# Working the later rows of the first batch before its earlier rows in a fused attention and two-MoE kernel

## The chip, the cores and the metric

The kernel runs on one core of a Trainium2 chip. The metric is the device time of one execution in microseconds (us); three executions of the kernel before were timed, and their median is the figure to compare with. Engines are called by the profile's names: PE is TensorE (PEld its weight loads), DVE is VectorE, ACT is ScalarE, POOL is GpSimd, SP is SyncE, whose queue issues most DMAs.

## What is computed

Four batches of attention over 8 heads, 576 rows and 64 columns a head, are followed by two MoE layers of 2304 rows, width 512 and inner width 2048.

```python
scores = scale * q @ k.T                  # causal: row i sees keys 0..i
local = softmax(scores) @ v
q_p = phi(q)                              # phi(x) = (x if x > 0 else exp(x) - 1) + 1
mem_out = (q_p @ M_prev) / (q_p . z_prev + 1e-6)
attn = sigmoid(beta) * mem_out + (1 - sigmoid(beta)) * local
x1 = silu(attn_rows @ w_in) @ w_out       # MoE 1
x2 = elu(x1 @ w2_in) @ w2_out             # MoE 2
```

The weights come as 64-bit floats.

## The kernel before, in words

**Attention.** The work of a batch is cut by pairs of heads (`NP` = 4 pairs) and by rows. Region "A" is rows 0 to 255 and needs keys 0 to 255; region "B" is rows 256 to 575 and needs all 576 keys. Batch 0 works A and B as tasks of their own (`tasks`, line 664), four A tasks and then four B tasks; batches 1 to 3 have tasks "AB" that do both. A task first loads q, k, v, the rows of q for the memory part, z and M (`load`), then makes its softmax (`soft`, called with "A", "23" or "4": the tiles of 128 rows, `wide` gives how many keys each sees) and its memory part (`mem_soft`), and, one task later in the program's order, turns the probabilities round on PE (`a_T`, `b_T`, into tile `a`), multiplies with v (`av_mm`) and ends with `av_end`, whose copy `pt<-av` is the last ACT instruction of a task and whose DMA writes the result to DRAM (`xdA`, `xdB`). In `soft`, ACT makes the exponentials with their sums, and for the tiles of region B also the scaling (`NORM`); for tile A the scaling is DVE's. Scores go into PSUM banks: tag "s" has two, and for the A tasks, which run only in batch 0, one bank is that of an accumulator ("acc0" or "acc1") of the MoE, which is not at work yet. Tiles `e3` and `e4` have one buffer a head, `eA` and `e2` two.

**MoE 1.** A block is 256 rows (all of "A", or two strips of 128 of "B"; the 64 rows left over of each batch make block "T"). Its x is read back from DRAM (`x_load`, tile `stg`) and cut in a high and a low part (`x`), so that three matmuls make one product of full precision. Eight steps j make the inner columns, two tiles of 128 each: `gemm1` writes `h`, ACT and DVE make `t` and `g`, `gemm2` adds into acc0 and acc1. The 32 weight tiles (16 of w_in, 16 of w_out, one of each by turns) are loaded with 512 KB each and decoded on ACT and DVE from 64-bit words (`w_value`, `w_split`: two ACT and four DVE instructions a tile); step j needs four of them. So that each decoded weight is used at once by two blocks, the first two blocks are worked in halves: block (0,A) with steps 0 to 3, block (0,B) with steps 0 to 3, (0,A) with steps 4 to 7, (0,B) with steps 4 to 7, and then block (1,A) whole. A block can't start before the last `av_end` of its region.

**Order.** All instructions are recorded first, and a planner (`Plan.order`) then sorts them: list scheduling forward and backward by turns with its own costs, and the best pass is taken. The program's order sets the first pass's priorities and, through the rotation of the tiles' buffers, a part of the dependences: q, k, v, z and M of a task go to buffers that an earlier task must have left. The first eight tasks have a bonus in priority (`BOOST`). When attention is over its buffers are given to the second part: the other six MoE 1 blocks in pairs, and MoE 2.

All instructions have line L199 (the planner's call), so groups are told apart by tile names. `h<-mask` are 70 filler matmuls of no use to the result.

Of the kernel before, what the change touches and what calls it, by code (L numbers as in the profile page):

```python
# [26 lines left out]
LAST = 3  # L27
# [361 lines left out]
def attention_moe_moe_kernel(  # L389
# [16 lines left out]
    B, H, D, S = qT.shape  # L406
    DM, DFF = w1_in.shape
    NF = DFF // 128
    NP = H // 2
# [20 lines left out]
    def new(pool, shape, dtype, tag, bufs=1):  # L430
        return nc.tile(pool, shape, dtype, tag, bufs, "psum" if pool is PP else "sbuf")

    def bank(tag, bufs=1):
        return new(PP, [128, 512], F32, tag, bufs)
# [226 lines left out]
        nc.vector.tensor_copy(pair[0:64, :], fv[0:64, :, 0])  # L661
        nc.vector.tensor_copy(pair[64:128, :], fv[64:128, :, 1])

    tasks = [(b, p, r) for b in range(B) for r in (("AB",) if b else ("A", "B")) for p in range(NP)]
    qk_t, pr_t, e_t, pq_t, pt_t = {}, {}, {}, {}, {}
    x_done = set()

# [42 lines left out]
    def scores(task, parts):  # L710

        rq, rk = qk_t[task]
        mm2([(outs[u], rq[u * 64:u * 64 + 64, q0:q1], rk[u * 64:u * 64 + 64, k0:k1], True, True)
             for outs, q0, q1, k0, k1 in parts for u in range(2)])

    def masked(o, s, m0, init, acc):
        m = mask[:, m0:m0 + o.shape[1]]
        nc.vector.tensor_tensor_reduce(out=o, in0=s, in1=m, scale=-scale, scalar=init,
                                       op0=ALU.add, op1=ALU.min, accum_out=acc)

    def soft(task, nms):


        b, p, rg = task
        heads = range(1 if nms == "4" else 2)
        k = 1 if nms == "4" else 2
        small = new(at, [128, 8], F32, f"sm{nms}", 2)
        mx, su = small[:, 0:4], small[:, 4:8]
        tiles = []
        for nm in nms:  # L730
            e = [new(at, [128, wide[nm]], F32, f"e{nm}{u}", 2 if nm in EDUP else 1) for u in heads]
            for u in heads:
                e_t[task, u, nm] = e[u]
            if nm == "4":
                ss, cn = [bank("s", 2) for _ in range(2)], ((0, 384), (384, 192))
                scores(task, [([s[0:64, 0:n], s[64:128, 0:n]], 512, 576, c, c + n) for s, (c, n) in zip(ss, cn)])
                for i in range(2):
                    s = ss[i]
                    c, n = cn[i]
                    masked(e[0][:, c:c + n], s[:, 0:n], (0, 512)[i], 3e38 if i == 0 else mx[:, 0:1], mx[:, i:i + 1])  # L740
                tiles.append((nm, e[0], 0, 576, 0, mx[:, 1:2]))
                continue
            s = [bank("s", 2), bank(f"acc{p % 2}") if rg == "A" else bank("s", 2)]
            parts = [(0, 0, 128, 0), (1, 128, 256, 1)] if nm == "A" else [(int(nm), 0, wide[nm], int(nm) - 2)]
            scores(task, [([s[u][:, off:off + n] for u in heads], qt * 128, qt * 128 + 128, 0, n)
                          for qt, off, n, c in parts])
            for u in heads:
                for qt, off, n, c in parts:
                    c += 2 * u
                    masked(e[u][:, off:off + n], s[u][:, off:off + n], 512 - n, 3e38, mx[:, c:c + 1])  # L750
                    tiles.append((nm, e[u], off, n, c, mx[:, c:c + 1]))
        for nm, e, off, n, c, m in tiles:
            nc.scalar.activation(e[:, off:off + n], e[:, off:off + n], AF.Exp, scale=-1.0, bias=m,
                                 accum_out=su[:, c:c + 1])
        k = len(heads)

        def cols(v):
            return v[:, 0:k * k].rearrange("p (u t) -> p u t", u=k)

        ogs = op[:, p:p + 1] if k == 1 else og[:, 2 * p:2 * p + 2]  # L760
        nc.vector.scalar_tensor_tensor(out=cols(su), in0=cols(su), scalar=1e-9,
                                       in1=ogs.unsqueeze(2).to_broadcast([128, k, k]), op0=ALU.add, op1=ALU.mult)
        nc.vector.reciprocal(out=mx[:, 0:k * k], in_=su[:, 0:k * k])
        for nm, e, off, n, c, m in tiles:
            if nm in NORM:
                nc.scalar.activation(e[:, off:off + n], e[:, off:off + n], AF.Copy, scale=mx[:, c:c + 1])
            else:
                nc.vector.tensor_scalar(out=e[:, off:off + n], in0=e[:, off:off + n], scalar1=mx[:, c:c + 1],
                                        scalar2=None, op0=ALU.mult)
# [92 lines left out]
    def s_items(task):  # L862
        b, p, rg = task
        it = [(lambda x=x: soft(task, x)) for x in {"A": ["A"], "B": ["23", "4"], "AB": ["A", "23", "4"]}[rg]]
        it.insert(1, lambda: mem_soft(task, rg[0]))
        return it
# [113 lines left out]
    def moe1(blks, nxt=None, **kw):  # L980
        blks = [x if len(x) == 3 else x + (None,) for x in blks]
        for i, (*blk, half) in enumerate(blks):
            blk = tuple(blk)
            while blk[1] != "T" and blk not in x_done:
                yield
            fetch(blk)
            raw = pre.pop(blk)
            n = blks[i + 1][:2] if i + 1 < len(blks) else nxt
            yield from moe1_block(blk, half, raw, mid=(lambda: fetch(n)) if n and n != blk else None, **kw)
# [12 lines left out]
    run(attention(0, n0, lambda: w_take(HOOK, W1A)))  # L1002
    w_take(W1A, W1A)
    order = [(b, r) for b in range(B) for r in "AB"] + [("T", "T")]
    first = [x + (h,) for h in (0, 1) for x in order[:2]] + order[2:LAST]
    g = moe1(first)
    calls = [0]

# [406 lines left out]
```

## Time and profile before

| | |
|---|---|
| median of 3 executions | 1000.48 us (1000.07 to 1001.79) |
| span of the profiled execution | 998.0 us, 2.5 us under that median |
| busy share of the span | PE 98%, PEld 84%, DVE 78%, ACT 66%, POOL 1% |
| mean granted TensorE clock | 0.997 |

The span runs from the first to the last instruction of one profiled execution; what is outside of it (the start and the end) is not in the trace. Busy time of PE is from modelled ends: matmuls are pipelined, and a busy PE needn't be at its peak. An idle time is given with what ended it.

### The profile page before, as it was taken

To read this page: it belongs to the slowest core of one execution; us is meant where nothing else is said; L and a number is where in the kernel's file an instruction comes from. 1 tells how busy PE (TensorE), PEld (TensorE's weight loads), DVE (VectorE), ACT (ScalarE), POOL (GpSimd) and SP (SyncE) were. 2 spreads that over 40 slices of the span, in tenths; PEclk is the share of its full clock that TensorE was granted. 3 is DMA by queue.
4 is the path that set the end of the run, shared out by engine and by line. 5 is a ranking of instruction groups with operands and counts; after the bars stand their busy time and mean duration, and the time that the engine had idled before them with its cause. 6 is when DMAs were issued, how large, how long until landed. Compare 5 with 4: busy or idle time off the path is not lost.

```text
span 998.0 us, 18153 instructions
## 1 busy us (share of the span) xinstructions
PE 981.4 (98%) x6582; PEld 837.5 (84%) x6582; DVE 782.1 (78%) x1887; ACT 663.6 (66%) x1507; POOL 9.3 (1%) x46
## 2 busy tenths in 40 slices
PE   8799999999999999999999999999999999999998
PEld 5378887777677899989889899889899999999897
DVE  7999998678767498689765989999889975656553
ACT  7999888788989655465555667666576644444433
POOL 1000000000000000000000000000000000000000
PEclk9999999999999999999999999999999999999999
DMA  8867753334332110033348555234235130303020
GB/s 250 231 185 233 224 165 111 112 96 118 104 96 80 41 51 2 22 107 128 125 130 272 190 191 169 88 104 147 76 115 168 43 128 1 127 1 107 1 64 22
DMA packets 107066, 115.36 MB, mean 116 GB/s; under 512 B 12000, under 2 KB 84192, under 8 KB 106976
## 3 DMA queue, kind: packets, MB, share of 16 engines
q1 hardware_dynamic: 106528, 113.67, 36.2%
q8 instruction: 52, 0.85, 0.4%
q10 hardware_dynamic: 448, 0.52, 0.1%
q14 instruction: 38, 0.31, 0.1%
HBM read 85.86 MB, written 28.31 MB: 114 GB/s over the span
## 4 chain that ended last, share of the span: by engine, by line
PE 90%; DVE 6%; ACT 2%; DMA 1%; issue 1%; SPq 0%; DVEq 0%; ACTq 0%
PE acc L199 24%; PE s L199 22%; PE tp L199 18%; PE h L199 14%; PE av L199 13%; DVE w L199 2%; ACT e L199 1%; DVE eA L199 1%; DVE e L199 1%; DVE qm L199 0%; ACT w L199 0%; DMA stg<-xdA 0%; DMA qm<-in_qn 0%; DVE ms L199 0%; DVE nm L199 0%
## 5 line engine op out<-in xcount | busy, mean ns | idle before, releaser
L199 PE MATMUL s<-x,w 128*128 128x256 f32 x1152 | 169.6, 282 | 0.0
L199 PEld LDWEIGHTS s<-x,w 128*128 128x128 f32 x1152 | 159.2, 190 | 8.8
L199 PE MATMUL acc<-g,w 128*128 128x256 f32 (+1 forms) x864 | 166.4, 326 | 0.0
L199 PEld LDWEIGHTS acc<-g,w 128*128 128x128 f32 x864 | 125.7, 190 | 13.3 <-issue 4.9
L199 PE MATMUL acc<-w,g 128*128 128x512 f32 x480 | 130.1, 393 | 0.0
L199 PE MATMUL tp<-x,w 128*128 128x256 f32 x816 | 117.1, 282 | 0.0
L199 PEld LDWEIGHTS tp<-x,w 128*128 128x128 f32 x816 | 108.3, 191 | 3.0
L199 ACT ACTIVATE e<-e,sm 128x384 f32<-128x384 f32 (+2 forms) x160 | 105.6, 689 | 3.8 <-DVE sm L199 3.0
L199 PEld LDWEIGHTS acc<-w,g 128*128 128x128 f32 x480 | 86.2, 189 | 13.9
L199 PE MATMUL h<-x,w 128*128 128x256 f32 x576 | 91.5, 296 | 0.6 <-DVE x L199 0.6
L199 ACT COPY x<-s 128x256 f32<-128x256 f32 x120 | 44.6, 372 | 61.3 <-PE s L199 57.3
L199 DVE SCALAR_TENSOR_TENSOR w<-w 128x512 int32<-128x512 int32 x124 | 83.9, 687 | 1.3
L199 PEld LDWEIGHTS h<-x,w 128*128 128x128 f32 x576 | 76.0, 190 | 6.2 <-issue 3.4
L199 ACT COPY a<-tp 128x384 f32<-128x384 f32 (+2 forms) x160 | 65.1, 424 | 11.4 <-PE tp L199 9.4
L199 ACT CAST g<-e 128x512 fp32r<-128x512 f32 (+1 forms) x80 | 46.0, 579 | 39.9 <-DVE e L199 39.7
L199 PE MATMUL s<-k,q 64*128 64x384 f32 (+5 forms) x368 | 68.6, 463 | 1.8 <-DMA k<-in_kT 1.1
L199 ACT ACTIVATE e<-h 128x512 f32<-128x512 f32 (+1 forms) x80 | 46.6, 589 | 29.5 <-DVE h L199 28.7
L199 DVE TENSOR_TENSOR g<-e,g 128x512 fp32r<-128x512 f32 (+1 forms) x80 | 50.3, 634 | 19.3 <-ACT g L199 18.5
L199 DVE SCALAR_TENSOR_TENSOR t<-t,h 128x512 f32<-128x512 f32 x72 | 49.1, 685 | 15.0 <-ACT t L199 14.8
L199 PE MATMUL tp<-ident,e 128*128 128x128 f32 x304 | 55.6, 284 | 5.3 <-ACT a L199 2.8
L199 ACT COPY x<-tp 128x512 f32<-128x512 f32 x56 | 32.9, 587 | 38.7 <-PE tp L199 38.2
L199 ACT CAST g<-t 128x512 fp32r<-128x512 f32 x72 | 44.6, 622 | 19.8 <-DVE t L199 18.8
(134 smaller groups left out, 1802.8 us busy)
## 6 DMA issues: line engine op xcount, KB each, us to landing
w<-in_moe_w_in SPq DMA_DIRECT2D x31, 512.0 KB, 4.3
w<-in_moe_w_out SPq DMA_DIRECT2D x31, 512.0 KB, 4.4
k<-in_kT SPq DMA_DIRECT2D x16, 288.0 KB, 4.0
y<-y SPq DMA_DIRECT2D x18, 256.0 KB, 2.5
qm<-in_qn SPq DMA_DIRECT2D x32, 128.0 KB, 2.9
vr<-in_vn SPq DMA_DIRECT2D x16, 256.0 KB, 3.7
w1s<-y SPq DMA_DIRECT2D x16, 256.0 KB, 2.0
w1s<-e SPq DMA_DIRECT2D x16, 256.0 KB, 2.3
```

The costliest lines, as they stand in the source:

```text
L199: r = getattr(issue, fn)(*[a.make() if isinstance(a, View) else a for a in args], **{k: v.make() if isinstance(v, View) else v for k, v in ...
```

## The change

Batch 0's tasks come in the order B, A; the first MoE 1 halves come in the order (0,B), (0,A), (0,B), (0,A). In the solo B tasks, the scores of tile "3" go to acc0 and acc1, and all scores of the solo A tasks to the two "s" banks.

```diff
-    tasks = [(b, p, r) for b in range(B) for r in (("AB",) if b else ("A", "B")) for p in range(NP)]
+    tasks = [(b, p, r) for b in range(B) for r in (("AB",) if b else ("B", "A")) for p in range(NP)]
...
-            s = [bank("s", 2), bank(f"acc{p % 2}") if rg == "A" else bank("s", 2)]
+            s = [bank(f"acc{u}") if rg + nm == "B3" else bank("s", 2) for u in range(2)]
...
-    first = [x + (h,) for h in (0, 1) for x in order[:2]] + order[2:LAST]
+    first = [x + (h,) for h in (0, 1) for x in order[1::-1]] + order[2:LAST]
```

## Rows read from the trace of the kernel before

**Rows 1.** The page's part 2: PE's busy tenths in 40 equal slices.
```profile
PE   8799999999999999999999999999999999999998
```

**Rows 2.** Busy us (instructions) by stretch: PE, PEld, DVE, ACT, POOL, clock, DMA share, GB/s.
```profile
10.00:33.00 23.00, 18.95 (x127) 10.83 (x127) 22.59 (x97) 21.39 (x63) 0.63 (x3) 1.00 0.87 261
33.00:51.00 18.00, 14.17 (x72) 6.85 (x73) 17.52 (x49) 16.80 (x42) 0.64 (x3) 0.91 0.79 228
51.00:89.00 38.00, 37.10 (x283) 28.27 (x281) 35.46 (x90) 37.80 (x89) 1.00 (x5) 1.00 0.64 202
89.00:110.00 21.00, 20.36 (x154) 16.62 (x153) 20.75 (x64) 18.45 (x47) 0.21 (x1) 1.00 0.64 190
110.00:164.00 54.00, 54.00 (x432) 47.97 (x432) 53.01 (x137) 45.41 (x108) 0.60 (x3) 1.00 0.59 179
...
200.00:344.00 144.00, 143.49 (x1071) 103.55 (x1069) 102.33 (x375) 128.15 (x352) 3.42 (x17) 1.00 0.31 89
```

**Rows 3.** The timeline of ACT: start, length; the last copy of some tasks.
```profile
33.17 0.39 ACT L199 COPY pt<-av 128x256 f32<-128x256 f32 x1
...
45.93 0.40 ACT L199 COPY pt<-av 128x320 f32<-128x320 f32 x1
...
63.75 0.43 ACT L199 COPY pt<-av 128x320 f32<-128x320 f32 x1
...
89.39 0.43 ACT L199 COPY pt<-av 128x320 f32<-128x320 f32 x1 [0.20 <-PE av L199]
```

**Rows 4.** The timeline of PE: scores, transposes, products and the first expert matmuls.
```profile
11.10 0.87 PE L199 MATMUL tp<-ident,eA 128*128 128x128 f32 x6
...
32.92 1.13 PE L199 MATMUL s<-k,q 64*128 64x512 f32 x4
...
35.36 1.30 PE L199 MATMUL av<-a,vr 128*64 128x320 f32 x8
...
47.06 0.94 PE L199 MATMUL tp<-ident,e 128*128 128x128 f32 x3 [1.46 <-ACT e L199]
...
50.82 0.36 PE L199 MATMUL h<-x,w 128*128 128x256 f32 x1
...
101.05 0.38 PE L199 MATMUL h<-x,w 128*128 128x256 f32 x1
```

**Rows 5.** Groups of ACT by form, 10 to 110 us: count, busy us, mean ns.
```profile
L199 ACT ACTIVATE e<-e,sm 128x512 f32<-128x512 f32 x20 | 14.0, 720 | 0.2 <-DVE sm L199 0.2
L199 ACT ACTIVATE w<-w 128x512 f32<-128x512 f32 x20 | 13.4, 684 | 0.0
...
L199 ACT CAST w<-w 128x512 fp32r<-128x512 f32 x19 | 12.0, 630 | 2.1 <-DVE w L199 2.1
...
L199 ACT ACTIVATE raw<-raw 128x512 f32<-128x512 f32 x1 | 0.7, 722 | 0.0
```

**Rows 6.** Groups of DVE by form, 10 to 110 us.
```profile
L199 DVE SCALAR_TENSOR_TENSOR w<-w 128x512 int32<-128x512 int32 x39 | 26.7, 688 | 0.2
...
L199 DVE COPY op<-og 64x4 f32<-64x4 f32 x1 | 0.2, 240 | 0.0
```

**Rows 7.** Groups of PE by form, 0 to 58 us.
```profile
L199 PE MATMUL tp<-ident,e 128*128 128x128 f32 x38 | 8.2, 316 | 4.6 <-ACT a L199 2.4 <-ACT e L199 2.2
...
L199 PE MATMUL s<-k,q 64*128 64x512 f32 x12 | 4.8, 807 | 0.0
...
L199 PE MATMUL av<-a,vr 128*64 128x320 f32 x24 | 4.1, 449 | 0.0
L199 PE MATMUL h<-x,w 128*128 128x256 f32 x24 | 3.9, 303 | 0.0
```

**Rows 8.** DMA issues, 0 to 60 us: count, KB each, median us to landing.
```profile
k<-in_kT SPq DMA_DIRECT2D x4, 288.0 KB, 4.2
...
k<-in_kT ACTq DMA_DIRECT2D x2, 128.0 KB, 3.1
```

**Rows 9.** PE's waits for a scores bank, whole span: us, times, longest.
```profile
PE s L199 <- DVE sm L199: 0.6, 1, 0.6
```

## The prediction

> **What bounds the kernel now.** I read the slices of the page first [rows 1]: PE is at 9 tenths or more in nearly all of the span, and what it lacks lies in the first four slices, 25 us each. So the end of the program is the PE's work plus what PE leaves unused early on; what is lost there isn't won back, because from some 60 us on PE always has more to do than time. Then I read the table by stretch [rows 2]: between 10 and 51 us PE is busy 33.1 of 41 us, while DVE is at 40.1 and ACT at 38.2; from 51 on PE is at 37.1 of 38 and then full. The early loss is thus not a lack of data: ACT and DVE, which make the softmax and decode the MoE weights at the same time, feed PE too slowly as long as attention alone is there to feed it. The PE timeline shows the turn [rows 4]: the first expert matmul starts at 50.82 us, some 18 us after the last A task has ended on ACT at 33.17 [rows 3]. From there PE has two sources, batch 0's B tasks and MoE 1, and fills up.
>
> So I ask one thing of the change: how much PE time is unused until the first expert matmul, and is PE full after it?
>
> **What one task costs.** For ACT I multiply the mean of each form by its count in a task. A B task has four exp or scaling instructions of 512 columns, four of 384, two of 576, the sums' reads, seven copies of `a`, and the memory part: 13.1 us. An A task has 5.1, a weight tile 0.684 + 0.630 = 1.31, an x split 1.6. Such durations overlap: the 25 rows of ACT between 10 and 110 us add up to 116 us [rows 5], where the four stretches there hold 94.4 us of busy time [rows 2]. So I scale by 0.81: B 10.6, A 4.1, weight 1.06, x 1.3. For DVE, 38 rows add to 116 too [rows 6] against 96.3, a factor of 0.83: B 6.3, A 4.8, weight 2.06, x 1.4. The eight tasks want 58.8 of ACT and 44.4 of DVE, whichever comes first, and 16 weight tiles (four steps of MoE 1) want 17 and 33. The engines' sums are alike, 76 and 77; only the order in which they turn into PE work differs.
>
> For PE I take the runs in its timeline [rows 4]: scores of 512 keys 1.13 us, six transposes 0.87, eight products of 320 rows 1.30. In proportion to columns and counts a B task is 3.2 of scores, 22 transposes 3.2, products 2.5, the end 0.5: 9.4 us. An A task is 0.85, eight transposes 1.2, 0.8 and 0.4: 3.2. Batch 0 is 50.4. These lengths include each run's last latency, so 10% less is the other end.
>
> **PE time unused before.** Up to 58 us PE has done [rows 7] all of A (12.8), the scores of three B tasks (12 of four each: 9.6), 38 of 19 transposes a task and two tasks' memory transposes (6.4), the products of two tasks (3.9 and 1.0) and 24 expert matmuls at 0.125 (432 in 54 us [rows 2]: 3.0): 36.7, so 21.3 us are unused. From 51 to 89 us it idles 0.9 more [rows 2]. At 77 us the loss stands at 22.2.
>
> **The change part by part.** *The start.* The first scores need 160 KB of q and 288 KB of k instead of 128 and 128. The median k of 288 KB lands after 4.2 us, those of 128 KB on ACT's queue after 3.1 [rows 8]: 1.1 us later, at most 2 if both early k transfers share the engines, at least 0 if other transfers gate. ACT's steady work starts at about 5.5 instead of 4.5. Each task issues the same DMAs as before, in another order on SP's queue and, for the first two k, ACT's. A B task brings 1 MB in some 14 us where an A task brought 0.6 in a third of that, so weights get through no later.
>
> *When B is done.* ACT is busy 96% between 10 and 89 us [rows 2]. Until the last B task ends it must do four B tasks (42.4), the decoding of some eight weights (8.5; two steps' worth, and DVE, with 6.3 us in a B task's 10.6, has room for them) and about one A task that runs ahead (4.1). 5.5 + 55.0 / 0.96 = 62.8 us. As a cross-check, before, the B tasks ended on average 14.5 us apart, from 45.93 to 89.39 [rows 3]; three such gaps behind a first task that ends at about 20 us give 63.5.
>
> *When MoE 1 starts.* Its x goes through DRAM. From a region's last copy to its first expert matmul it took 17.6 us for A (33.17 to 50.82) and 11.7 for B (89.39 to 101.05) [rows 3, 4]: 14.6 on average, so 77.4 us, with 74.5 and 80.4 as the ends. This handoff is the crux: before, it was covered by B tasks, which give PE 9.4 us for 10.6 of ACT; now it is covered by A tasks, 3.2 for 4.1. By ACT's sum, 5.5 + (58.8 + 9 x 1.06 + 1.3) / 0.96 = 78 us, all of attention is just done when the handoff is over, and nothing else can have fed PE.
>
> *The sum.* At 77.4 us PE has done batch 0's attention and no more: 77.4 - 50.4 = 27.0 us unused, 4.8 more than before. With PE's pieces 10% shorter it is 32.0 against 25.6, 6.4 more. I take 5.5.
>
> *What comes back.* Behind that point PE has expert matmuls without B tasks between them. In 51 to 89 us, with both, 7.4 matmuls started in a microsecond, in 110 to 164, mostly experts, 8.0 [rows 2]: 38 x (1 - 7.4 / 8.0) = 2.8 us. Part of it is only that attention has longer matmuls; between nothing and 2.8 I take 1.4. Weights can't starve PE much: nine are there, a step of one block is 48 matmuls, 6 us, and wants four more weights, 8.2 of DVE, but block (0,A) follows some 14 us later and uses the decoded ones again.
>
> *The banks.* Tile 3's scores get banks of their own, so they needn't wait for tile 2's masks. PE waited for a scores bank 0.6 us in the whole span [rows 9]; that is the bound of this gain, and of the loss to A, whose two heads now share the "s" pair. I take nothing: ACT stands ahead of it. If the cover went, scores of the next task would queue on PE behind it. The accumulator banks are free long before the first block. POOL's zeroing of `a` moves along and has no one waiting in a row here.
>
> 998.0 + 5.5 - 1.4 = 1002.1 us of span; the runs' median lies 2.5 above the profiled span, so 1004.5 us (1004.6, rounded).
>
> **The clock, and a rule that speaks against the change.** The granted clock is 0.91 in 33 to 51 us and 1.00 around it [rows 2]: about 1.6 us of full-speed time were lost at the half level (1.2 of 2.4 GHz), after PE had sat 1.46 us until an exponential came [rows 4]. The Trainium skill, "TensorE: Matmul & The Clock Gate", section "HAM oscillation — how this bites in real kernels", says that a PE which keeps pausing for its data falls back to the half clock and works its next burst cold. The trace agrees in that one place; by that rule a stretch of attention alone that lasts 77 us instead of 51 would meet it more often, say twice more, and the sum would be 1004.5 + 3.2 = 1007.7. My sum leaves it at nothing more, since PE isn't the bound there, and the slow rival has room for it.
>
> **The rivals.** *Faster.* The planner may hold back weights and A. With four weights and no A, B ends at 5.5 + (42.4 + 4.2) / 0.96 = 54 us, and MoE starts at 65.8 with the short handoff. PE then has four B tasks and 2.7 A tasks, 46.2 us, and 19.6 unused, against 21.3 + 0.2 before: 1.9 less, and the whole 2.8 comes back: 995.8. For it: the planner sorts freely among work that is ready, and DVE has time for weights beside B. Against it: only four weights serve one step, and DVE is as full as ACT by 94 us. It decides from an MoE start below some 71 us.
>
> *Equal.* ACT and DVE have the same sums to about 100 us, where batch 0's attention and 16 weights must be done in either order, and in 200 to 344 us, where ACT is at 89% and matmuls start only 7.4 a microsecond [rows 2], a few us of expert matmuls left over may slip in without making it longer. Then 1000.5. Against it: PE counts as full there.
>
> *Much slower.* `e3` and `e4` have one buffer, so a B task's third tile waits for all transposes of the task before. If B tasks end 16 us apart (before, one gap was 17.8 [rows 3]), the last ends at 68, MoE starts at 82.6, and 32.2 us are unused: 9.8 more than the 22.4 that it would have been before, less 1.4: 1008.9.
>
> *No change at all* is excluded: the planner sorts again, but tasks take the buffers of q, k, v and `e` in the program's order, so A can't slip past B.
>
> **Numbers.** Forecast (2 to 7 us slower) 0.37, much slower 0.15, equal 0.20, faster 0.28. The forecast's own range is 1002.5 to 1007.5; for 8 in 10 I reach to 996 and 1011. A change under 0.2% (2 us) can't be told from none here. Faster by more 0.28, within 0.20, slower by more 0.52.
>
> **What would show it.** Right: the first expert matmul at 74 to 81 us; the last 320-row `pt<-av` of batch 0 near 63; ACT near 96% until then; PE idle mostly in 60 to 77; the rest of the trace as before, some 4 us later. Wrong: an expert matmul before 71 us, PE fuller before 60 us than the task costs allow, or the attention's end, at 344 us before, not moved at all, which would mean that ACT, not PE, sets that stretch.

## The result and the profile after

The changed kernel takes 1009.5 us (median of 4 executions, 1008.23 to 1009.94) where the kernel before took 1000.28 in the same series: a ratio of 1.0092, 95% interval 1.008 to 1.0105. It is slower, as forecast, but by 9.2 us and not by 4.0: the time lies above the forecast's own range (1002.5 to 1007.5) and inside the wide one (996 to 1011), and the size is more than double the forecast. The span of the profiled execution went from 998.0 to 1008.2.

The table by stretch of the kernel after, with the columns and stretches of [rows 2]:

```profile
10.00:33.00 23.00, 19.17 (x130) 10.32 (x130) 16.75 (x55) 21.52 (x52) 0.40 (x2) 1.00 0.68 224
33.00:51.00 18.00, 14.24 (x94) 7.88 (x92) 15.83 (x50) 17.88 (x45) 0.81 (x4) 1.00 0.58 163
51.00:89.00 38.00, 31.34 (x194) 20.64 (x194) 35.60 (x125) 33.09 (x96) 1.02 (x5) 0.91 0.69 205
89.00:110.00 21.00, 21.00 (x163) 18.62 (x163) 20.68 (x58) 15.38 (x38) 0.21 (x1) 1.00 0.72 216
110.00:164.00 54.00, 54.00 (x420) 45.05 (x417) 52.63 (x148) 47.74 (x117) 0.60 (x3) 1.00 0.61 184
200.00:344.00 144.00, 144.00 (x1078) 107.04 (x1076) 98.93 (x360) 124.69 (x333) 3.24 (x16) 1.00 0.31 93
```

Against [rows 2], PE's busy time is the same up to 51 us; then it misses 5.8 us of busy time in 51 to 89 (31.34 for 37.10), with 89 matmuls fewer. DVE has lost time early: 32.6 of 41 us where it had 40.1. ACT is at least as full as it was up to 51 us and has room later.

The last copies of batch 0's tasks on ACT (start, length; 320 rows are B, 256 are A); here, as in [rows 3], a task's end is told by the start of this copy:

```profile
28.34 0.43 ACT L199 COPY pt<-av 128x320 f32<-128x320 f32 x1
...
41.54 0.42 ACT L199 COPY pt<-av 128x320 f32<-128x320 f32 x1
...
54.56 0.43 ACT L199 COPY pt<-av 128x320 f32<-128x320 f32 x1
...
65.91 0.42 ACT L199 COPY pt<-av 128x320 f32<-128x320 f32 x1
...
69.69 0.36 ACT L199 COPY pt<-av 128x256 f32<-128x256 f32 x1
...
77.77 0.37 ACT L199 COPY pt<-av 128x256 f32<-128x256 f32 x1
...
85.40 0.37 ACT L199 COPY pt<-av 128x256 f32<-128x256 f32 x1
...
98.93 0.35 ACT L199 COPY pt<-av 128x256 f32<-128x256 f32 x1
```

And the first expert matmuls on PE:

```profile
76.75 1.11 PE L199 MATMUL h<-x,w 128*128 128x256 f32 x3
...
77.95 0.36 PE L199 MATMUL h<-x,w 128*128 128x256 f32 x1
...
79.35 2.89 PE L199 MATMUL h<-x,w 128*128 128x256 f32 x20
```

B ends at 65.9 (62.8 forecast), the first expert matmul comes at 76.75 and steadily from 79.35 (77.4 forecast; 50.82 before [rows 4]). Two markers of both kernels tell when the loss is complete: the activation of MoE 1's fourth step, and the last copy of the last attention task.

The timeline of ACT of the kernel before, and under it that of the kernel after:

```profile
91.48 0.59 ACT L199 ACTIVATE t<-h 128x512 f32<-128x512 f32 x1
...
344.36 0.43 ACT L199 COPY pt<-av 128x320 f32<-128x320 f32 x1 [1.68 <-PE av L199]
```
```profile
101.34 0.60 ACT L199 ACTIVATE t<-h 128x512 f32<-128x512 f32 x1 [1.56 <-PE h L199]
...
354.38 0.43 ACT L199 COPY pt<-av 128x320 f32<-128x320 f32 x1 [1.56 <-PE av L199]
```

The fourth step is 9.9 us later; the last attention task ends at 354.4 instead of 344.4, 10.0 later; the span ends 10.2 later. All of the loss arises before 101 us, and none of it comes back.

### The profile page after: what moved, and what is told of

The parts are those of the page before. It is cut to its first block, busy times and chain, and to the rows that moved or that the text cites. A ratio compares the mean times of both kernels' runs of the same rounds, so it can differ in the third digit from the quotient of the medians.

```text
span 1008.2 us, 18153 instructions
## 1 busy us (share of the span) xinstructions
PE 987.8 (98%) x6582; PEld 840.2 (83%) x6582; DVE 784.7 (78%) x1887; ACT 665.5 (66%) x1507; POOL 9.3 (1%) x46
## 4 chain that ended last, share of the span: by engine, by line
PE 92%; ACT 4%; DVE 3%; DMA 1%; issue 1%; SPq 0%; DVEq 0%
PE acc L199 25%; PE s L199 22%; PE tp L199 18%; PE h L199 14%; PE av L199 13%; ACT e L199 2%; ACT a L199 1%; ACT w L199 1%; DVE w L199 1%; DVE e L199 1%; DMA zb<-in_z_prev 0%; DMA sm<-in_beta 0%; DVE eA L199 0%; DVE nm L199 0%; ACT pt L199 0%
## 5 line engine op out<-in xcount | busy, mean ns | idle before, releaser
L199 PE MATMUL acc<-g,w 128*128 128x256 f32 (+1 forms) x864 | 168.6, 327 | 0.0
L199 PE MATMUL h<-x,w 128*128 128x256 f32 x576 | 87.4, 294 | 0.4 <-DVE t L199 0.2
L199 PE MATMUL tp<-ident,e 128*128 128x128 f32 x304 | 58.1, 287 | 7.0 <-ACT e L199 3.5
L199 PE MATMUL s<-k,q 64*128 64x384 f32 (+4 forms) x368 | 64.4, 451 | 0.4 <-DVE sm L199 0.2
L199 PEld LDWEIGHTS tp<-ident,e 128*128 128x128 f32 x304 | 36.0, 142 | 29.3 <-ACT a L199 9.6
```

The source lines that it names most:

```text
L199: r = getattr(issue, fn)(*[a.make() if isinstance(a, View) else a for a in args], **{k: v.make() if isinstance(v, View) else v for k, v in ...
```

## The experiments

Sixteen kernels ran, each beside the kernel before on its chip (999.8 to 1000.0 us there). The table has the start of the 24th expert matmul, read in the PE timeline: with it the `h` of MoE 1's first step is complete, and a few early ones don't mislead. The planner sorts each kernel anew, so a run differs from its neighbour by more than its edit.

| kernel | us | ratio to before (95%) | 24th expert matmul at |
|---|---|---|---|
| before | 1000.3 | | 56.2 |
| after | 1009.5 | 1.0092 (1.008 to 1.0105) | 82.0 |
| e1 tasks only | 1016.5 | 1.0163 (1.0147 to 1.0178) | 103.3 |
| e2 MoE order only | 1017.35 | 1.0165 (1.0148 to 1.0182) | 104.2 |
| e3 s banks | 1020.4 | 1.0197 (1.0182 to 1.0213) | 91.3 |
| e4 fillers | 1012.6 | 1.0125 (1.011 to 1.014) | 87.5 |
| e5 pairs, after | 1007.9 | 1.0078 (1.0063 to 1.0093) | 80.9 |
| e6 pairs, before | 1000.0 | 1.0001 (0.9991 to 1.001) | 51.8 |
| e7 scaling on DVE, after | 1006.8 | 1.0069 (1.0054 to 1.0084) | 79.2 |
| e8 scaling on DVE, before | 1006.15 | 1.0062 (1.0047 to 1.0077) | 62.0 |
| e9 free, after | 1000.4 | 1.0007 (0.9997 to 1.0016) | 31.5 |
| e10 free, before | 995.9 | 0.9961 (0.9947 to 0.9976) | 39.7 |
| e11 other plan, after | 1008.4 | 1.0088 (1.0072 to 1.0105) | 82.2 |
| e12 other plan, before | 1000.7 | 1.0009 (0.9999 to 1.0018) | 62.6 |
| e13 free and DVE, after | 1001.6 | 1.0016 (1.0007 to 1.0025) | 35.5 |
| e14 free and DVE, before | 1005.0 | 1.0052 (1.0035 to 1.0069) | 46.9 |
| e15 POOL scales weights, after | 1014.3 | 1.0144 (1.0129 to 1.0159) | 87.7 |
| e16 POOL scales weights, before | 1002.1 | 1.0023 (1.0014 to 1.0033) | 60.1 |

**Half of the change at a time.** e1 keeps the changed tasks and takes the old order of MoE 1's blocks; e2 the other way round.

```diff
 # e1, from the kernel after
-    first = [x + (h,) for h in (0, 1) for x in order[1::-1]] + order[2:LAST]
+    first = [x + (h,) for h in (0, 1) for x in order[:2]] + order[2:LAST]
 # e2, from the kernel before: the same line the other way
```

> Batch 0's tasks in the changed order (B, A), MoE 1 in the old order, block (0,A) first. Theory 1 (the loss is PE's unused time until the first expert matmul, at 76.8 us in the changed kernel): the first expert matmul now waits for the last A task (98.9 us) and some 12 us of handoff, so 105 to 112 us; part of the gap goes to batch 1's attention; 1018 to 1032 us. Rival 2 (the long B tasks in front cost by themselves, through banks or buffers, and the MoE's start matters little): 1007 to 1012.

> Batch 0's tasks in the old order (A, B), the MoE 1 halves in the changed order, (0,B) first. Theory 1: the first expert matmul waits for the last B task, which ends earlier than before (89 us) as MoE 1 no longer shares ACT and DVE, at 74 to 80, plus 12: 86 to 92 us; PE has only attention until then; 1009 to 1016 us. Rival 2 (B tasks in front are what costs): like the kernel before, 999 to 1003.

The PE timeline of e1, and under it that of e2:

```profile
100.14 3.47 PE L199 MATMUL h<-x,w 128*128 128x256 f32 x24 [0.83 <-ACT x L199]
```
```profile
100.91 3.55 PE L199 MATMUL h<-x,w 128*128 128x256 f32 x24 [0.48 <-ACT x L199]
```

In both, the first expert matmul now waits for a region that is finished last, and comes at the same time, 100 and 101 us. The two have opposite orders of attention and take the same time, 1016.5 and 1017.35. So B in front, with the banks that go with it, isn't dear by itself: e2 has A in front and loses 17 us. What counts is when MoE 1 can start. Both starts missed their forecasts, e1 5 us earlier than 105 and e2 9 later than 92; e1's time is just under its range and e2's just over. From the changed kernel to e1 the start moves 21 us and the time 7, from the kernel before to e2 48 and 17, so a microsecond of waiting costs about a third of one. Batch 1's attention fills a part: its first 256-row copy comes at 100.9 us in e1 and at 122.3 in the changed kernel.

**The banks.** e3 has all scores in the two "s" banks.

```diff
-            s = [bank(f"acc{u}") if rg + nm == "B3" else bank("s", 2) for u in range(2)]
+            s = [bank("s", 2) for u in range(2)]
```

> The changed kernel, but with all scores in the two s banks and none in the accumulators' banks. Theory 1: the banks carry nothing, 1007.5 to 1011.5. Rival 3 (the banks' new use makes or hides a wait): more than 3 us away from 1009.5, slower if the banks of their own help, faster if they bind.

The last B task's end in e3, on ACT:

```profile
72.73 0.42 ACT L199 COPY pt<-av 128x320 f32<-128x320 f32 x1
```

And e3's only wait of PE for a scores bank, whole span:

```profile
PE s L199 <- DVE sm L199: 0.2, 1, 0.2
```

It ends 6.8 us later than with the banks (65.91), MoE 1 starts 9 later, and the kernel takes 10.9 us more than the changed one (medians; the profiled execution of e3 was the fastest of its four, 1017.66). Rival 3 holds here, and my zero for the banks was wrong: they don't cause the loss, they hide a second one of that size. The 0.6 us of waits in [rows 9] did not bound it, and e3 itself shows only 0.2 us of them: what the banks are worth does not appear as PE's wait for one. By what way they act is not shown.

**The clock.** In 50 to 60 us the changed kernel's granted clock was 0.69; e4 puts 230 more filler matmuls in PE's pauses up to the first expert matmul.

```diff
-NFILL = 70
+NFILL = 300
```

> The changed kernel with 300 filler matmuls instead of 70; they stand all the way to the first expert matmul and keep PE from pausing, so that the granted clock should stay at 1.00 where it was 0.69 in 50 to 60 us. Theory 1: PE isn't the bound there, at most 1.5 us come back: 1008 to 1010. Rival 4 (the half clock is a main part of the loss): 3 us or more come back, 1006.5 or less, first expert matmul before 74 us.

The table by stretch, 50 to 60 us of the kernel after, then 50 to 80 us of e4, and last the end of B's last task in e4's ACT timeline:

```profile
50.00:60.00 10.00, 8.27 (x35) 4.55 (x37) 9.39 (x32) 9.41 (x26) 0.20 (x1) 0.69 0.48 148
```
```profile
50.00:80.00 30.00, 25.86 (x242) 18.30 (x239) 28.52 (x112) 27.03 (x82) 1.02 (x5) 0.98 0.69 203
```
```profile
67.72 0.42 ACT L199 COPY pt<-av 128x320 f32<-128x320 f32 x1
```

The first cut of MoE 1's x on ACT, in the kernel after and under it in e4:

```profile
75.76 0.40 ACT L199 CAST x<-stg 128x256 fp32r<-128x256 f32 x1
```
```profile
79.58 1.02 ACT L199 CAST x<-stg 128x256 fp32r<-128x256 f32 x3 [0.26 <-DMA stg<-xdB]
```

The clock stayed up (0.98; 1.00 in 10 to 50), yet the last B task ended at 67.72 and not earlier than 65.91: there is no sign that PE's clock paces the B tasks. The kernel got 3 us slower, which neither theory 1 nor rival 4 had, and MoE 1 started 5.5 later. Most of that is the way of x: ACT could begin to cut it only at 79.58, when its DMA had landed, 3.8 us later than in the kernel after; of these 1.8 are B's later end, the rest isn't explained. That the fillers stood in PE's way is not shown. A pure price of the half clock isn't to be had from this run; that it is a main part of the loss is excluded only so far as B's pace goes.

**The handoff.** e5 and e6 read batch 0's x back pair by pair.

```diff
+                for k in range(4 if b == 0 else 0):
+                    nc.sync.dma_start(raw[:, k, i * 128:(i + 1) * 128], xd[blk][k, :, c:c + 128])
...
```

> The changed kernel, but batch 0's x is read back from DRAM pair by pair (eight DMAs of 64 KB for a block instead of two of 256 KB), so that three quarters of it can be there before the last task of the region ends. Theory 1 (each us by which the first expert matmuls come earlier gives back some 0.4 to 0.5 us, as PE's unused time grows by 4.8 us in 70 to 80 us): expert matmuls 4 to 6 us earlier, 1006 to 1008.5. Rival 5 (the handoff is not what holds MoE 1 back, but the decoded weights or ACT): within 1 us of 1009.5.

> The kernel before with the same reading back pair by pair. Theory 1: expert matmuls at 43 to 47 us instead of 50.8, but B tasks are there to fill PE and only four weights are decoded, so 0 to 3 us come back: 997 to 1000. Rival 5: unchanged, 999.5 to 1000.5.

After the change 1.6 us come back, which is not clear of noise (the intervals of e5 and of the kernel after overlap, and another plan alone moved 1.1, e11); in the kernel before nothing, though there the 24th expert matmul starts 4.4 us earlier: while B tasks fill PE, an earlier start is worth nothing. In e5 some matmuls ran early, but the 24th came only 1.1 earlier, not 4 to 6, because the last pair's way through DRAM remained: its x landed at 75.6 us, where all of x landed by 75.7 in the kernel after.

**The engines' fit.** e7 and e8 let DVE scale the probabilities of batch 0's B tasks.

```diff
-            if nm in NORM:
+            if nm in NORM and rg != "B":
```

> The changed kernel, but in batch 0's B tasks DVE scales the probabilities instead of ACT. Theory 6 (in the changed order ACT paces the B tasks at 96% while DVE is at 31.6 of 40 us in 10 to 50 us, so the two engines' work no longer fits together): some 2.4 us less ACT a task, the last B task ends 5 to 8 us earlier, expert matmuls 4 to 7 earlier, 1005 to 1008. Rival 7 (the chain of one B task through its single buffers paces them): last B task within 2 us of 65.9, 1008.5 to 1011.

> The kernel before with the same move of scaling from ACT to DVE in batch 0's B tasks. Theory 6: there both engines are full between 10 and 50 us (38.1 and 39.1 of 40), so nothing is gained, 999 to 1003. Rival 7: nothing either, so this run bounds what the move itself does.

The stretch 10 to 50 us of the kernel after, then of e7 and of e8:

```profile
10.00:50.00 40.00, 32.41 (x214) 17.52 (x214) 31.58 (x99) 38.39 (x93) 1.00 (x5) 1.00 0.64 198
```
```profile
10.00:50.00 40.00, 35.13 (x229) 19.03 (x227) 39.10 (x122) 33.96 (x88) 1.20 (x6) 0.96 0.72 221
```
```profile
10.00:50.00 40.00, 31.05 (x182) 16.55 (x182) 39.29 (x144) 33.06 (x93) 1.45 (x6) 0.95 0.75 222
```

The end of B's last task in e7:

```profile
63.83 0.43 ACT L199 COPY pt<-av 128x320 f32<-128x320 f32 x1
```

In the changed order the move fills DVE (31.6 to 39.1) and gives back 2.7 us; in the old one, where DVE was full, it costs 6.2, more than the 3 that I allowed. So in the changed order DVE has time to spare and ACT is the fuller engine. That ACT paces the B tasks is not shown: with 4.4 us less of it in 10 to 50 the last one ended only 2.1 us earlier, not the 5 to 8 of theory 6 and hardly more than the 2 of rival 7, and the 24th expert matmul came 2.8 earlier, not 4 to 7.

**Without the wait.** e9 and e10 take the x of the first halves of blocks (0,A) and (0,B) from the input q, so MoE 1 waits only for weights. The work is the same; the output isn't the reference's.

```diff
+        if b == 0 and blk not in given:
+            given.add(blk)
...
+                    nc.sync.dma_start(raw[:, k, i * 128:(i + 1) * 128],
+                                      qT[0, 2 * k:2 * k + 2, :, c:c + 128].rearrange("h d s -> (h d) s"))
```

> The changed kernel, but the first halves of MoE 1's blocks (0,B) and (0,A) take their x from the input q instead of attention's result, so they need not wait for it (the output is not the reference's, the work is the same). Theory 1 (the loss is the wait of MoE 1 for a whole region): the expert matmuls start as soon as weights are decoded, and the time falls to within 3 us of the kernel before with the same edit, 995 to 1001. Theory 6 alone (the engines' work fits together worse in this order whatever MoE 1 waits for): it stays 4 us or more above that kernel.

> The kernel before with the same edit, x of the first halves from the input q (output not the reference's). Theory 1: the unused time before 50 us shrinks a little, as weights bound the first steps: 994 to 999. Theory 6: the same.

The changed order gains 9.1 us, the old one 4.4. The distance shrinks from 9.2 to 4.5: the wait makes some 5 us of the loss, and 4.5 remain, which is 1.5 more than theory 1 allowed and within what theory 6 asked for (4 or more). By the third of a microsecond from e1 and e2, the start that came 25.8 us later would make the whole 9.2; the two readings are not reconciled. The stretches of e9, and under them those of e10:

```profile
0.00:30.00 30.00, 24.57 (x171) 15.54 (x173) 20.56 (x69) 23.02 (x56) 2.38 (x12) 1.00 0.77 234
...
50.00:110.00 60.00, 56.67 (x432) 45.71 (x431) 59.05 (x187) 52.23 (x141) 1.73 (x8) 1.00 0.70 211
```
```profile
0.00:30.00 30.00, 24.55 (x186) 15.73 (x186) 24.00 (x115) 24.15 (x77) 3.05 (x14) 1.00 0.77 228
...
50.00:110.00 60.00, 59.93 (x454) 50.02 (x454) 59.51 (x152) 54.77 (x128) 1.00 (x5) 0.99 0.74 231
```

DVE does 3.4 us less up to 30 us in e9 and is nearly full from then on in both; PE misses 3.3 us in 50 to 110.

**What the rest is.** e13 and e14 join e9's and e10's edit with the move of scaling; e15 and e16 let POOL make the first ACT instruction of the first ten weight tiles.

```diff
+        if made_w[0] <= 10:
+            nc.gpsimd.tensor_scalar(out=f32(hi_w), in0=f32(hi_w), scalar1=2.0 ** -112, scalar2=None, op0=ALU.mult)
...
```

> The changed kernel with both edits: the first halves of blocks (0,B) and (0,A) take x from the input q (output not the reference's), and DVE scales the probabilities of batch 0's B tasks. Theory 6 (the 4.5 us that were left when MoE 1 did not wait come from DVE's time that goes unused early, beside an ACT that is full): 2.5 to 4.5 us below 1000.4, so 996 to 998. Rival 9 (what was left has to do with the A tasks coming late, or with the later plan): 999 to 1002.

> The kernel before with the same two edits (output not the reference's). Theory 6: DVE is full there from the start, so the move costs as it did without the first edit, 4 to 8 us above 995.9: 1000 to 1004. Rival 9: within 2 us of 995.9.

> The changed kernel, but POOL instead of ACT makes the first of the two ACT instructions of the first ten weight tiles (scaling by a power of two), 0.68 us each; no work is added for DVE. Theory 10 (in the changed order ACT is full with B tasks and keeps weights from DVE, which has 8 us free in 10 to 50): DVE busier in 10 to 50, more weights decoded at 77 us than 8, 2 to 5 us back: 1004 to 1007.5. Rival 11 (DVE's early time can't be used, since B's own order sets it): within 1.5 us of 1009.

> The kernel before with the same edit. Theory 10: DVE is full there, and the ten instructions less on ACT give at most 2 us: 998 to 1000.5. Rival 11: the same, 999 to 1001.

e13 gives nothing back (1001.6 against 1000.4): theory 6, as put there, fell, and rival 9's range was met, with two doubts: the move also hands DVE work in a kernel where DVE is full later, and the granted clock was 0.83 in 10 to 50 us of e13 where it was 1.00 in e9. In the old order the same move cost 9.1 us there (e14 against e10), more than the 4 to 8 expected. In e15 DVE was fuller early, 38.1 of 40 us, and ten instead of eight weights were decoded at 77 us, but B's last task ended 3.9 us later, MoE 1 started 5.7 later and the kernel took 4.8 more. So here more weights early didn't help; theory 10 fell too, with a doubt: POOL took 1.70 us an instruction, where ACT takes 0.68, and DVE was slower beside it. In the old order the same edit cost 2 us (e16), which neither expectation had. The groups by form: POOL in e15 over the whole span, then DVE in e15 in 10 to 50 us, and last DVE's same group and stretch in the kernel after:

```profile
L199 POOL TENSOR_SCALAR w<-w 128x512 f32<-128x512 f32 x10 | 16.9, 1696 | 27.1 <-DMA w<-in_moe_w_in 16.1 <-DMA w<-in_moe_w_out 4.8 <-DVE sm L199 3.1
```
```profile
L199 DVE TENSOR_SCALAR w<-w 128x512 int32<-128x512 int32 x8 | 4.9, 614 | 0.0
```
```profile
L199 DVE TENSOR_SCALAR w<-w 128x512 int32<-128x512 int32 x6 | 2.6, 426 | 0.0
```

**The plan's luck.** e11 and e12 change only the planner's margin.

```diff
-SLACK = 150.0
+SLACK = 130.0
```

> The changed kernel with the planner's margin SLACK at 130 instead of 150 ns, which changes nothing but the order that it settles on. All theories: 1009.5 within 3 us. Rival 8 (the loss is an unlucky plan): 1004 or less.

> The kernel before with SLACK at 130 instead of 150 ns. All theories: 1000.3 within 3 us. Rival 8 (the kernel before owes its time to a lucky plan): 1005 or more.

1008.4 and 1000.7: this other plan moves either kernel by about 1 us, not by 9.

No run with the reference's output was faster than the kernel before.

## Why the prediction was right in sign and wrong in size

**Right.** The start: the median k of 288 KB on ACT's queue landed after 4.2 us, 1.1 more than before, as put. B's end was 3.1 us late, with ACT at 38.4 of 40 us (96%) in 10 to 50. The handoff took 10.8 us to the first expert matmul and 13.4 to the steady ones (14.6 forecast), and they started within 2 us of 77.4. PE's idle time lay near where it was put, 4.0 of the 11 us from 66 to 77. That the start of MoE 1 is what costs is shown by e1 and e2 together; e9 and e10 put some 5 of the 9 us on it. That B tasks cover it in the old order fits e6, where an earlier start gave nothing.

**The step that failed** is the last one of *When MoE 1 starts*, on which *The sum* rests: "all of attention is just done when the handoff is over, and nothing else can have fed PE". At 77.4 us one of the four A tasks had ended; the others ended at 77.8, 85.4 and 98.9, not at 78. The predicted extra loss there was 5.5; measured at the fourth step it is 9.9. Of the 4.4 between, 2.0 is the later steady start (79.35). The rest is an estimate from a count of PE's work in the trace: at 79.35 us 8 transposes and the products and ends of two A tasks were still to do, 3.6 us by the prediction's costs, and PE had done 1.4 of other work instead (batch 1's first scores and four expert matmuls), so 2.2 us.

Why the A tasks came late is argued from two rows and not tested by itself. I summed ACT alone. DVE, with 4.8 us for an A task, had let 7.5 us go by up to 51 us, when ACT was full of B, and was then the fuller engine of the stretch in which the last three A tasks ended (after; columns as in [rows 2]):

```profile
77.00:99.00 22.00, 21.39 (x167) 18.73 (x166) 21.17 (x56) 15.69 (x40) 0.62 (x3) 1.00 0.66 196
```

The two engines' sums were equal, as I wrote; my reading is that equal sums fit in the same time only if the work of both is there together: A and weights for DVE beside B for ACT, as in the old order. e13 and e15, which gave DVE more to do early, did not bear this out, each with its doubts.

**Also wrong:** *What comes back*, 1.4 us, was nothing (9.9 at the fourth step, 10.2 at the end). *The banks*, priced at nothing, are worth 10.9 us in this order (e3): without them the change would have cost 20. And the slices [rows 1] show PE under 9 tenths in the first two of 25 us, not in the first four.

**The rivals.** *Much slower* gave 1008.9, near the time, by a mechanism that didn't happen: B tasks ended 13.2, 13.0 and 11.4 us apart, not 16. *Equal* hoped that later stretches would absorb the rest; attention ended 10.0 us later instead. *Faster* needed MoE 1 to start before 71 us. The half clock did come up for longer (0.69 in 50 to 60 us, 0.57 in 53 to 61), and the paragraph on it, with 1007.7, lay nearer than my sum; but no run shows what it costs here, and e4 shows no gain from lifting it.

**Open** is what makes the 4.5 us that stay when MoE 1 doesn't wait. DVE's 3.4 us lost before 30 us and PE's 3.3 in 50 to 110 agree in size, but neither run that gave DVE more early (e13, e15) brought them back.

## What to carry to other kernels

Before reordering stages, ask what covers each handoff: a stage that others wait for belongs where much PE work of another kind is ready beside it, here the cheap A tasks first, so that the dear B tasks cover the way of x through DRAM. Sums of engine time decide only if the engines' shares match in each stretch; two stages that fill different engines are better tried side by side than one after the other, though how much of the loss here is due to that stayed open. A wait measured in one order is no bound for a buffer's worth in another.

## What was not expected of the hardware

POOL's scaling of 128x512 strided float32 took 1.70 us by the profile, whose spans on POOL are rough, two and a half times ACT's 0.68. DVE's shift of the same tiles went from 426 to 614 ns on average, and only where POOL ran beside it: of the eight shifts in 10 to 50 us of e15, the four that overlapped a POOL scaling took 0.73 to 0.87 us, the four others 0.40 to 0.42. The granted clock stood at the half level for about 6 of the 10 us from 50 to 60 (0.69 is 62% of the stretch at half), after PE had run single transposes from 51.8 us on with pauses of 0.2 to 0.6 us before them, all of them waits for ACT's `e`.
